# Retention attention feeding a GELU feed-forward layer: two units per attention block, q/k transposes by DMA, state summed in SBUF, initial loads reordered

## The chip, the cores and the metric

The kernel runs on one core of one Trainium2 chip. The metric is the device time of one execution in microseconds. The core has the engines PE (TensorE matmul, with its weight loads shown apart as PEld), DVE (VectorE), ACT (ScalarE), POOL (GpSimd) and SP (SyncE). In this kernel POOL and SP mostly issue DMAs.

## The reference, cut to what matters

```python
# q, k, v: batch 8, heads 8, sequence 576, head width 64
scores = scale * q @ k.T                        # per batch and head
gamma  = 1 - 2 ** (-5 - head)
Dmat   = where(i >= j, gamma ** (i - j), 0)     # decay, causal
attn   = (scores * Dmat) @ v
x = attn.transpose(0, 2, 1, 3).reshape(4608, 512)
h = x @ w_in                                    # 512 -> 2048
out = (h * sigmoid(1.702 * h)) @ w_out          # 2048 -> 512
```

The decay splits into a factor of the row and a factor of the column, so a sequence can be worked off in pieces of 128 positions: within a piece by masked scores, and from all earlier pieces through a running state, the sum of k times the scaled v.

## The kernel before, in words

**Units and chunks.** The 4608 rows are cut into 36 units of 128 rows (`NU`). Nine units make two batches: units 0 to 3 are pieces 0 to 3 of the first batch (kind 0), units 4 to 7 those of the second (kind 1), and the ninth holds the last 64 positions of both (kind 2). Four units are one chunk of 512 rows for the feed-forward part, so there are 9 chunks.

**One unit of attention.** `load_qk` and `load_v` bring k, q (cast to bf16 on the way) and v (fp32) to SBUF in rows of positions; all are issued from POOL. `scale_v` (DVE, L284) multiplies v by the column's decay into `vp`. `transposes` (L293) turns k and q with eight 128x128 transposes on PE into the PSUM bank `psT`, and one DVE copy (L296) brings them to `qkT`. `state` (L305) adds the four head pairs' k-v products to the bank `psK`, where they accumulate over the pieces of a batch; `state_out` (L315) multiplies the bank by a block-diagonal mask `bdm` into `kv`. `inter` (L326, or L332 for the ninth units) multiplies q by that state into `psO`; it is absent for the first piece of a batch. `scores` (L342) makes the eight heads' scores with half-height (64-row) matmuls into two banks `psS`, `scores_out` (L350) masks them into `pm`, `values` (L359) adds `pm` times `vp` to `psO` with half-width (64-column) matmuls, and `values_out` (L368) applies the row's decay and writes 128 columns of `xT`.

**Feed-forward.** `up` (L374) is four 512-column matmuls and a GELU on ACT (L379) into `gT`; 16 of them make a chunk. `down` (L392) is four 512-column matmuls, a quarter of one unit's output; after four of them `down_out` copies the bank on ACT (L401) to `osb` and SP stores it.

**Order.** Every engine takes its instructions in program order; `Program` adds the semaphore waits. One loop step `t` deals with one unit: state of unit `t`, transposes of `t+2`, inter of `t`, scores of `t+1`, values of `t`, then four `up` groups of an earlier chunk and four `down` groups of a still earlier one (`LAG` = 12 steps behind), one of each in turn. The first `up` is at step 4, the first `down` at step 12. POOL issues the loads in this order: k, q, v of units 0 to 3, and then alternately a quarter of `w_in` and the three loads of one further unit, and later `w_out`.

Of the kernel before, what the change touches and what calls it, by code (L numbers as in the profile page):

```python
# [7 lines left out]
ALU = mybir.AluOpType  # L8
# [5 lines left out]
P = 128  # L14
# [5 lines left out]
LAG = 12  # L20
# [121 lines left out]
def bass_retnet_parallel__then__act_gelu_quick_kernel(  # L142
# [8 lines left out]
    NLD = 8  # L151
    es = ExitStack()
    with es:
# [10 lines left out]
        bdm = sb("bdm", [P, P], BF16)  # L164
# [6 lines left out]
        qn = [sb(f"qn{i}", [P, H, DH], BF16) for i in range(NLD)]  # L171
        kn = [sb(f"kn{i}", [P, H, DH], BF16) for i in range(NLD)]
        vn = [sb(f"vn{i}", [P, H, DH], FP32) for i in range(NLD)]
        vp = [sb(f"vp{i}", [P, H, DH], BF16) for i in range(3)]
        qkT = [sb(f"qkT{i}", [P, 2 * HP, P], BF16) for i in range(3)]
        pm = [[sb(f"pm{i}_{hh}", [P, HP, P], BF16) for hh in range(2)] for i in range(2)]
        kv = [[sb(f"kv{i}_{j}", [P, HP, P], BF16) for j in range(2)] for i in range(2)]
# [3 lines left out]
        gT = [sb(f"gT{i}", [P, NF, 512], BF16) for i in range(4)]  # L181
        osb = [sb(f"osb{i}", [P, DM], FP32) for i in range(4)]

        psT = ps("psT", [P, 2 * HP, P], BF16)
        psS = [ps(f"psS{hh}", [P, HP, P]) for hh in range(2)]
        psO = ps("psO", [P, HP, P])
        psK = ps("psK", [P, HP, P])
        psH = [ps(f"psH{i}", [P, 512]) for i in range(2)]
        psY = ps("psY", [P, 512])
# [4 lines left out]
        def load_qk(u):  # L194
            sl = u % NLD
            rows = unit_rows(u)
            for src, dst, nm in ((k, kn[sl], "kn"), (q, qn[sl], "qn")):
                def f(e, src=src, dst=dst):
                    return [
                        e.dma_start(  # L200
                            dst[p0 : p0 + n, :, :],
                            src[b, :, s0 : s0 + n, :].rearrange("h p d -> p h d"),
                        )
                        for p0, n, b, s0 in rows
                    ]
                op("pool", f, writes=[f"{nm}{sl}"], dma=f"d_{nm}{sl}", ndma=len(rows))

        def load_v(u):
# [11 lines left out]
            op("pool", f, writes=[f"vn{sl}"], dma=f"d_vn{sl}", ndma=len(rows))  # L220
# [13 lines left out]
        def setup():  # L234
# [3 lines left out]
            op("pool", lambda e: e.iota(  # L238
                iota_c.ap(), [[1, S]], base=0, channel_multiplier=0,
                allow_small_or_imprecise_dtypes=True), writes=["iota_c"])  # L240
            op("pool", lambda e: e.iota(
                iota_k.ap(), [[128, 5]], base=0, channel_multiplier=1,
                allow_small_or_imprecise_dtypes=True), writes=["iota_k"])
            op("dve", lambda e: e.tensor_scalar_add(
                iota_k[64:128, 4:5], iota_k[64:128, 4:5], -64.0),
               reads=["iota_k"], writes=["iota_k"])
            op("dve", lambda e: e.tensor_single_scalar(ident.ap(), dmat.ap(), 0.0, ALU.is_equal),  # L247
               reads=["dmat"], writes=["ident"])
            op("dve", lambda e: e.tensor_single_scalar(mask.ap(), dmat.ap(), 0.0, ALU.is_ge),
               reads=["dmat"], writes=["mask"])  # L250
            op("dve", lambda e: e.tensor_single_scalar(maskc.ap(), dmat.ap(), 0.0, ALU.is_ge),
               reads=["dmat"], writes=["maskc"])
            op("dve", lambda e: e.memset(maskc[0:64, 64:128], 0.0), reads=["maskc"], writes=["maskc"])
            op("dve", lambda e: e.memset(bdm.ap(), 0.0), writes=["bdm"])
            op("dve", lambda e: e.memset(bdm[0:64, 0:64], 1.0), reads=["bdm"], writes=["bdm"])
            op("dve", lambda e: e.memset(bdm[64:128, 64:128], 1.0), reads=["bdm"], writes=["bdm"])
            op("dve", lambda e: e.memset(lnsc.ap(), math.log(QK_SCALE)), writes=["lnsc"])
            for hp in range(HP):
                for hh in range(2):
                    op("dve", lambda e, hp=hp, hh=hh: e.memset(  # L260
                        lng[64 * hh : 64 * hh + 64, hp : hp + 1], math.log(gamma(2 * hp + hh))),
                       writes=[f"lng{hp}_{hh}"])
            for h in range(H):
# [18 lines left out]
        def scale_v(u):  # L282
            sl, _, ty = u % NLD, *unit_info(u)[1:]
            op("dve", lambda e: e.tensor_tensor(  # L284
                vp[u % 3].ap(), vn[sl].ap(),
                vfac[:, ty, :, None].to_broadcast([P, H, DH]), ALU.mult),
               reads=[f"vn{sl}"] + VF, writes=[f"vp{u % 3}"])

        def transposes(u):
            sl = u % NLD  # L290
            for t, (src, nm) in enumerate(((kn[sl], "kn"), (qn[sl], "qn"))):
                for hp in range(HP):
                    op("pe", lambda e, src=src, hp=hp, t=t: e.matmul(  # L293
                        psT[:, (1 - t) * HP + hp, :], src[:, 2 * hp : 2 * hp + 2, :], ident.ap(),
                        is_transpose=True), reads=[f"{nm}{sl}", "ident"], writes=["psT"])
            op("dve", lambda e: e.tensor_copy(qkT[u % 3].ap(), psT.ap()),  # L296
               reads=["psT"], writes=[f"qkT{u % 3}"])

        def state(u):
# [3 lines left out]
            sl = u % NLD  # L303
            for hp in range(HP):
                op("pe", lambda e, hp=hp: e.matmul(  # L305
                    psK[:, hp, :], kn[sl][:, 2 * hp : 2 * hp + 2, :],
                    vp[u % 3][:, 2 * hp : 2 * hp + 2, :],
                    start=(c == 0 and hp == 0), stop=True, skip_group_check=True),
                   reads=[f"kn{sl}", f"vp{u % 3}"], writes=["psK"])

# [206 lines left out]
```

## Time and profile before

| what | value |
|---|---|
| time, median of 3 runs (range) | 338.47 us (338.08 to 339.63) |
| the profiled execution | 338.57 us, its span 336.7 us |
| PE busy | 316.9 us, 94% of the span |
| DVE, ACT, POOL busy | 132.6, 115.4, 108.5 us |
| first `up` on PE | 33.80 us |
| end of the last matmul | 332.8 us |
| chain that ended last | PE 89%, POOL 6%, DMA 3% |

The profile is of one execution. The span runs from the first to the last recorded instruction; the time is 1.9 us longer. Matmuls are pipelined, so the length of one matmul says less than the distance from one start to the next.

### The profile page before, as it was taken

How to read it: one execution, taken by the hardware profiler on the slowest of the kernel's cores; microseconds unless marked ns; L12 is line 12 of the kernel's file. 1: busy time of each engine (PE TensorE's matmuls, PEld its weight loads, DVE VectorE, ACT ScalarE, POOL GpSimd, SP SyncE). 2: the span in 40 equal slices, each digit the busy share in tenths (PEclk: the TensorE clock that was granted, in tenths of full speed). 3: DMA queues.
4: the chain of work that ended last, by engine and by line, in shares of the span. 5: the costliest groups of instructions: out<-in, count | busy, mean ns of one | idle time of the engine just before them, and what ended most of it. 6: DMA issues, size and time to landing. Idle time of an engine off the chain costs nothing.

```text
span 336.7 us, 5221 instructions
## 1 busy us (share of the span) xinstructions
PE 316.9 (94%) x2272; PEld 162.5 (48%) x2272; DVE 132.6 (39%) x229; ACT 115.4 (34%) x198; POOL 108.5 (32%) x135
## 2 busy tenths in 40 slices
PE   1676999999999999999999999999999999999995
PEld 0444455555555555555555555555555544443442
DVE  2687766864444434444444434444443200000000
ACT  5400345443333333333333333333333344442211
POOL 8999976842322514222322604000000000000000
PEclk9999999999999999999999999999999999999999
DMA  9999999996666907667666907001000001011122
GB/s 83 190 196 218 215 210 214 221 202 88 98 88 86 153 31 98 91 95 93 95 93 94 158 31 95 31 33 31 33 31 33 31 34 62 31 33 62 62 94 64
DMA packets 87447, 32.85 MB, mean 98 GB/s; under 512 B 76416, under 2 KB 80512, under 8 KB 87424
## 3 DMA queue, kind: packets, MB, share of 16 engines
q0 software_dynamic: 82176, 23.08, 60.3%
q1 hardware_dynamic: 5248, 9.44, 8.1%
q8 instruction: 18, 0.29, 0.4%
q14 instruction: 5, 0.04, 0.0%
HBM read 36.70 MB, written 9.44 MB: 137 GB/s over the span
## 4 chain that ended last, share of the span: by engine, by line
PE 89%; POOL 6%; DMA 3%; ACT 0%; issue 0%; POOLq 0%
PE psH L374 38%; PE psY L392 31%; PE psS L392 4%; PE psT L293 4%; PE psO L359 3%; DMA qn<-in_q_dram 3%; PE psS L342 3%; PE psO L392 2%; POOL kn L200 2%; PE psK L305 2%; POOL vn L214 2%; POOL qn L200 2%; PE psO L326 1%; POOL w_in_sb L223 1%; ACT osb L401 0%; PE psO L332 0%
## 5 line engine op out<-in xcount | busy, mean ns | idle before, releaser
L379 ACT ACTIVATE gT<-psH 128x512 bf16<-128x512 f32 x144 | 86.0, 597 | 182.9 <-PE psH L374 182.9
L374 PE MATMUL psH<-xT,w_in_sb 128*128 128x512 bf16 x576 | 145.1, 381 | 0.0
L392 PE MATMUL psY<-w_out_sb,gT 128*128 128x512 bf16 x480 | 122.2, 379 | 0.7 <-ACT osb L401 0.7
L374 PEld LDWEIGHTS psH<-xT,w_in_sb 128*128 128x128 bf16 x576 | 52.6, 98 | 65.4 <-ACT gT L379 5.1
L392 PEld LDWEIGHTS psY<-w_out_sb,gT 128*128 128x128 bf16 x480 | 46.5, 98 | 57.9 <-ACT osb L401 2.4
L296 DVE COPY qkT<-psT 128x1024 bf16<-128x1024 bf16 x36 | 24.8, 690 | 108.0 <-PE psT L293 107.9
L200 POOL DMA_DIRECT2D kn<-in_k_dram x40 | 36.8, 928 | 94.8 <-PE psK L305 80.3
L214 POOL DMA_DIRECT2D vn<-in_v_dram x40 | 37.4, 947 | 2.5 <-issue 2.4
L200 POOL DMA_DIRECT2D qn<-in_q_dram x40 | 37.0, 935 | 0.0
L284 DVE TENSOR_TENSOR vp<-vn,vfac 128x512 bf16<-128x512 f32 x36 | 24.6, 685 | 13.9 <-DMA vn<-in_v_dram 13.9
L368 DVE TENSOR_TENSOR xT<-psO,gq 128x512 bf16<-128x512 f32 x36 | 24.5, 680 | 6.0 <-PE psO L359 6.0
L293 PE MATMUL psT<-ident,kn 128*128 128x128 bf16 x144 | 15.5, 236 | 11.3 <-DVE ident L247 5.2
L401 ACT ACTIVATE osb<-psY 128x512 f32<-128x512 f32 x30 | 17.9, 597 | 14.0 <-PE psY L392 14.0
L350 DVE TENSOR_TENSOR pm_1<-psS,mask 128x512 bf16<-128x512 f32 x32 | 21.8, 680 | 0.0
L350 DVE TENSOR_TENSOR pm_0<-psS,mask 128x512 bf16<-128x512 f32 x32 | 21.8, 680 | 0.0
L293 PE MATMUL psT<-ident,qn 128*128 128x128 bf16 x144 | 15.5, 236 | 1.5 <-DMA qn<-in_q_dram 1.5
L293 PEld LDWEIGHTS psT<-ident,kn 128*128 128x128 bf16 x144 | 10.4, 105 | 13.3 <-DMA kn<-in_k_dram 8.6
L359 PE MATMUL psO<-pm_1,vp 128*64 128x128 bf16 x144 | 15.9, 237 | 0.0
L359 PE MATMUL psO<-pm_0,vp 128*64 128x128 bf16 x144 | 15.9, 237 | 0.0
L342 PE MATMUL psS<-qkT 64*128 64x128 bf16 x288 | 15.6, 233 | 0.0
L305 PE MATMUL psK<-vp,kn 128*128 128x128 bf16 x128 | 13.5, 233 | 2.0 <-DVE kv_0 L315 1.4
L305 PEld LDWEIGHTS psK<-vp,kn 128*128 128x128 bf16 x128 | 10.0, 103 | 9.6 <-DVE kv_0 L315 1.9
(44 smaller groups left out, 140.3 us busy)
## 6 DMA issues: line engine op xcount, KB each, us to landing
vn<-in_v_dram POOLq DMA_DIRECT2D x32, 256.0 KB, 5.0
out_dram<-osb SPq DMA_DIRECT2D x32, 256.0 KB, 2.0
kn<-in_k_dram POOLq DMA_DIRECT2D x32, 128.0 KB, 4.5
qn<-in_q_dram POOLq DMA_DIRECT2D x32, 128.0 KB, 5.2
w_in_sb<-in_moe_w_in_dram POOLq DMA_DIRECT2D x4, 512.0 KB, 10.1
w_out_sb<-in_moe_w_out_dram POOLq DMA_DIRECT2D x4, 512.0 KB, 15.5
vn<-in_v_dram POOLq DMA_DIRECT2D x8, 128.0 KB, 6.3
out_dram<-osb SPq DMA_DIRECT2D x8, 128.0 KB, 2.4
```

The lines of the kernel that those rows point to most:

```text
L200: e.dma_start(dst[p0 : p0 + n, :, :], src[b, :, s0 : s0 + n, :].rearrange("h p d -> p h d"),)
L214: e.dma_start(vn[sl][p0 : p0 + n, :, :], v[b, :, s0 : s0 + n, :].rearrange("h p d -> p h d"),)
L284: op("dve", lambda e: e.tensor_tensor(vp[u % 3].ap(), vn[sl].ap(), vfac[:, ty, :, None].to_broadcast([P, H, DH]), ALU.mult), reads=[f"vn{s ...
L293: op("pe", lambda e, src=src, hp=hp, t=t: e.matmul(psT[:, (1 - t) * HP + hp, :], src[:, 2 * hp : 2 * hp + 2, :], ident.ap(), is_transpose= ...
L296: op("dve", lambda e: e.tensor_copy(qkT[u % 3].ap(), psT.ap()), reads=["psT"], writes=[f"qkT{u % 3}"])
L305: op("pe", lambda e, hp=hp: e.matmul(psK[:, hp, :], kn[sl][:, 2 * hp : 2 * hp + 2, :], vp[u % 3][:, 2 * hp : 2 * hp + 2, :], start=(c == 0 ...
L342: op("pe", lambda e, hp=hp, hh=hh: e.matmul(psS[hh][:, hp, :], qt[64 * hh : 64 * hh + 64, HP + hp, :], qt[64 * hh : 64 * hh + 64, hp, :], ...
L350: op("dve", lambda e, hh=hh: e.tensor_tensor(pm[u % 2][hh].ap(), psS[hh].ap(), m[:, None, :].to_broadcast([P, HP, P]), ALU.mult), reads=[f ...
L359: op("pe", lambda e, hp=hp, hh=hh: e.matmul(psO[64 * hh : 64 * hh + 64, hp, :], vp[u % 3][:, 2 * hp + hh, :], pm[u % 2][hh][:, hp, :], sta ...
L374: op("pe", lambda e, a=a: e.matmul(psH[n % 2].ap(), w_in_sb[:, a, P * f : P * f + P], xT[c % 3][:, a, :], start=(a == 0), stop=(a == HP - 1)),
L379: op("act", lambda e: e.activation(gT[c % 4][:, f, :], psH[n % 2].ap(), AF.Gelu_apprx_sigmoid), reads=[f"psH{n % 2}"], writes=[f"gT{c % 4} ...
L392: op("pe", lambda e, f=f: e.matmul(y, gT[c % 4][:, f, P * r : P * r + P], w_out_sb[:, f, :], start=(f == 0), stop=(f == NF - 1)), reads=[f ...
```

## The change

Units 0 to 7 get an attention of their own (`attend`), one unit after the other with all its steps in a row: units 0 to 3 before the first chunk's 16 `up`, units 4 to 7 between that chunk and the next. In these the transposes stay on PE and the copy alternates between DVE (even units) and ACT (odd units). From unit 8 on, `block(m)` takes two units at a time, `2m` and `2m+1`: both `inter`, then the `scores` of the next two units, then both `values`. The transposes of units 8 to 35 are one DMA each, from SBUF to SBUF, issued by SP two blocks ahead (`ready`). k and q share the tile `kq`. The state is no longer accumulated in PSUM: each piece's product goes to a bank of its own, and DVE adds its two diagonal halves to an fp32 sum `kvf` in SBUF and copies that to `kv` in bf16 (`state`); the off-diagonal parts of the eight `kv` tiles are zeroed once at the start. Between blocks a written-out plan of eight `up` and eight `down` groups is run, with the states of the two units after next at its fourth and seventh `up`. v is loaded from SP, and the order of the first loads is k and q of units 0 to 3, all of `w_in`, k and q of units 4 to 7, then `w_out`, while the v loads on SP wait for named earlier loads. Banks and buffers are renamed and counted anew. In `scores` the two units of a pair use banks `S0`, `S1` and `S2`, `S3`; `S0` and `S2` also take `down`'s output, and `S1` the states.

```diff
-LAG = 12
...
+    NQT = 10
+    NVP = 6
+    NPE = 8
...
-        bdm = sb("bdm", [P, P], BF16)
...
-        qn = [sb(f"qn{i}", [P, H, DH], BF16) for i in range(NLD)]
-        kn = [sb(f"kn{i}", [P, H, DH], BF16) for i in range(NLD)]
+        kq = [sb(f"kq{i}", [P, 2, DM], BF16) for i in range(NLD)]
         vn = [sb(f"vn{i}", [P, H, DH], FP32) for i in range(NLD)]
-        vp = [sb(f"vp{i}", [P, H, DH], BF16) for i in range(3)]
-        qkT = [sb(f"qkT{i}", [P, 2 * HP, P], BF16) for i in range(3)]
-        pm = [[sb(f"pm{i}_{hh}", [P, HP, P], BF16) for hh in range(2)] for i in range(2)]
-        kv = [[sb(f"kv{i}_{j}", [P, HP, P], BF16) for j in range(2)] for i in range(2)]
+        vp = [sb(f"vp{i}", [P, H, DH], BF16) for i in range(NVP)]
+        qkT = [sb(f"qkT{i}", [P, 2 * HP, P], BF16) for i in range(NQT)]
+        pm = [[sb(f"pm{i}_{hh}", [P, HP, P], BF16) for hh in range(2)] for i in range(4)]
+        kvf = [sb(f"kvf{i}", [P, HP, DH], FP32) for i in range(2)]
+        kv = [[sb(f"kv{i}_{j}", [P, HP, P], BF16) for j in range(4)] for i in range(2)]
...
-        gT = [sb(f"gT{i}", [P, NF, 512], BF16) for i in range(4)]
+        gT = [sb(f"gT{i}", [P, NF, 512], BF16) for i in range(3)]
...
-        psT = ps("psT", [P, 2 * HP, P], BF16)
-        psS = [ps(f"psS{hh}", [P, HP, P]) for hh in range(2)]
-        psO = ps("psO", [P, HP, P])
-        psK = ps("psK", [P, HP, P])
-        psH = [ps(f"psH{i}", [P, 512]) for i in range(2)]
-        psY = ps("psY", [P, 512])
+        banks = {n: ps(f"ps{n}", [P, 512]) for n in ("H0", "H1", "O0", "O1", "S0", "S1", "S2", "S3")}
+
+        def by_pair(n):
+            return banks[n].ap().rearrange("p (a b) -> p a b", b=P)
...
+        def load_v(u, after=()):
...
-            op("pool", f, writes=[f"vn{sl}"], dma=f"d_vn{sl}", ndma=len(rows))
+            op("sp", f, reads=after, writes=[f"vn{sl}"], dma=f"d_vn{sl}", ndma=len(rows))
...
+            for i in range(2):
+                for j in range(4):
+                    op("dve", lambda e, i=i, j=j: e.memset(kv[i][j].ap(), 0.0), writes=[f"kv{i}_{j}"])
...
+        def transpose_pe(u, bank):
             sl = u % NLD
-            for t, (src, nm) in enumerate(((kn[sl], "kn"), (qn[sl], "qn"))):
-                for hp in range(HP):
-                    op("pe", lambda e, src=src, hp=hp, t=t: e.matmul(
-                        psT[:, (1 - t) * HP + hp, :], src[:, 2 * hp : 2 * hp + 2, :], ident.ap(),
-                        is_transpose=True), reads=[f"{nm}{sl}", "ident"], writes=["psT"])
-            op("dve", lambda e: e.tensor_copy(qkT[u % 3].ap(), psT.ap()),
-               reads=["psT"], writes=[f"qkT{u % 3}"])
-
-        def state(u):
+            t = banks[bank].ap().bitcast(BF16).rearrange("p (a b) -> p a b", b=P)
+            for j in range(2 * HP):
+                op("pe", lambda e, j=j: e.matmul(
+                    t[:, j, :], kq[sl][:, j // HP, P * (j % HP) : P * (j % HP) + P], ident.ap(),
+                    is_transpose=True), reads=[f"kq{sl}_{j // HP}", "ident"], writes=[bank])
+            if u % 2:
+                op("act", lambda e: e.activation(qkT[u % NQT].ap(), t, AF.Copy),
+                   reads=[bank], writes=[f"qkT{u % NQT}"])
+            else:
+                op("dve", lambda e: e.tensor_copy(qkT[u % NQT].ap(), t),
+                   reads=[bank], writes=[f"qkT{u % NQT}"])
+
+        def transpose_dma(u):
+            sl = u % NLD
+            op("sp", lambda e: e.dma_start_transpose(
+                qkT[u % NQT].ap(), kq[sl].ap().rearrange("p a b -> p (a b)")),
+               reads=[f"kq{sl}_0", f"kq{sl}_1"], writes=[f"qkT{u % NQT}"],
+               dma=f"d_qkT{u % NQT}")
...
+        def state(u, bank="S1"):
             pb, kind, c = unit_info(u)
             if kind == 2:
                 return
             sl = u % NLD
+            kb = by_pair(bank)
             for hp in range(HP):
                 op("pe", lambda e, hp=hp: e.matmul(
-                    psK[:, hp, :], kn[sl][:, 2 * hp : 2 * hp + 2, :],
-                    vp[u % 3][:, 2 * hp : 2 * hp + 2, :],
-                    start=(c == 0 and hp == 0), stop=True, skip_group_check=True),
-                   reads=[f"kn{sl}", f"vp{u % 3}"], writes=["psK"])
-
-        def state_out(u):
-            pb, kind, c = unit_info(u)
-            if kind == 2:
-                return
-            op("dve", lambda e: e.tensor_tensor(
-                kv[kind][c % 2].ap(), psK.ap(), bdm[:, None, :].to_broadcast([P, HP, P]), ALU.mult),
-               reads=["psK", "bdm"], writes=[f"kv{kind}_{c % 2}"])
+                    kb[:, hp, :], kq[sl][:, 0, P * hp : P * hp + P],
+                    vp[u % NVP][:, 2 * hp : 2 * hp + 2, :],
+                    start=(hp == 0), stop=True, skip_group_check=True),
+                   reads=[f"kq{sl}_0", f"vp{u % NVP}"], writes=[bank])
+            for hh in range(2):
+                r = slice(64 * hh, 64 * hh + 64)
+                dst, acc, src = kv[kind][c][r, :, r], kvf[kind][r], kb[r, :, r]
+                kvk, kfk = f"kv{kind}_{c}_{hh}", f"kvf{kind}_{hh}"
+                if c == 0:
+                    op("dve", lambda e, d=acc, s=src: e.tensor_copy(d, s), reads=[bank], writes=[kfk])
+                elif c < 3:
+                    op("dve", lambda e, d=acc, s=src: e.tensor_tensor(d, s, d, ALU.add),
+                       reads=[bank, kfk], writes=[kfk])
+                if c < 3:
+                    op("dve", lambda e, d=dst, s=acc: e.tensor_copy(d, s),
+                       reads=[kfk, f"kv{kind}_{c}"], writes=[kvk])
+                else:
+                    op("dve", lambda e, d=dst, s=src, a=acc: e.tensor_tensor(d, s, a, ALU.add),
+                       reads=[bank, kfk, f"kv{kind}_{c}"], writes=[kvk])
...
+        def attend(u, tbank, kbank):
+
+            scale_v(u)
+            transpose_pe(u, tbank)
+            state(u, kbank)
+            scores(u)
+            scores_out(u, 0)
+            scores_out(u, 1)
+            inter(u)
+            values(u)
+            values_out(u)
+
+        def fetch(m):
+            for u in (2 * m, 2 * m + 1):
+                if u < NU:
+                    load_kq(u)
+                    load_v(u)
+
+        def ready(m):
+            for u in (2 * m, 2 * m + 1):
+                if u < NU:
+                    scale_v(u)
+                    transpose_dma(u)
+
+        def block(m):
+
+            a, b = 2 * m, 2 * m + 1
+            nxt = 2 * m + 2 < NU
+            inter(a)
+            inter(b)
+            if nxt:
+                scores(a + 2)
+                scores(b + 2)
+                scores_out(a + 2, 0)
+            values(a)
+            values(b)
+            values_out(a)
+            values_out(b)
+            if nxt:
+                scores_out(a + 2, 1)
+                scores_out(b + 2, 0)
+                scores_out(b + 2, 1)
+            fetch(m + 4)
+            ready(m + 2)
+
+        def states(m, i):
+            u = 2 * m + (i == 6)
+            if i in (3, 6) and u < NU:
+                state(u)
+
+        YB = ("S0", "S2")
+
+        load_kq(0)
         setup()
         load_v(0)
         for u in range(1, 4):
-            load(u)
+            load_kq(u)
+            load_v(u, [f"kq{u - 1}_1"])
         for i in range(4):
             load_win(i)
-            load(4 + i)
-        nh = 0
-        for t in range(-2, NU + LAG):
-            if t + 2 < NU:
-                scale_v(t + 2)
-            if 0 <= t < NU:
-                state(t)
-            if t + 2 < NU:
-                transposes(t + 2)
-            if 0 <= t < NU:
-                state_out(t)
-                inter(t)
-                if t < 4:
-                    load_wout(t)
-                load(t + NLD)
-            if 0 <= t + 1 < NU:
-                scores(t + 1)
-                scores_out(t + 1)
-            if 0 <= t < NU:
-                values(t)
-                values_out(t)
-            ch, hq = divmod(t - 4, 4)
-            co, r = divmod(t - LAG, 4)
-            bank = "psY"
-            if t >= NU + 4:
-                bank = ("psY", "psS0", "psS1", "psO")[t % 4]
-            for s in range(4):
-                if 0 <= ch < NCH:
-                    up(ch, 4 * hq + s, nh)
-                    nh += 1
-                if 0 <= co < NCH:
-                    down(co, r, s, bank)
-            if 0 <= co < NCH:
-                down_out(co, r, bank)
+        for u in range(4, 8):
+            load_kq(u)
+            load_v(u, [f"win{2 + (u > 5)}"])
+        for u in range(4):
+            attend(u, "H0", "H1")
+        for i in range(4):
+            load_wout(i)
+        fetch(4)
+        for f in range(16):
+            up(0, f)
+        for u in range(4, 8):
+            attend(u, "O0", "S3")
+        ready(4)
+        fetch(5)
+        for f in range(16):
+            up(1, f)
+            states(4, f - 8)
+        ready(5)
+        scores(8)
+        scores(9)
+        for u in (8, 9):
+            for hh in range(2):
+                scores_out(u, hh)
+        fetch(6)
+        for i in range(8):
+            down(0, i, ("S0", "S2"))
+        fetch(7)
+        block(4)
+        for i in range(8, 16):
+            down(0, i, ("S0", "S2"))
+            states(5, i - 8)
+        for m in range(5, NU // 2 + 1):
+            if m < NU // 2:
+                block(m)
+            c, h = divmod(m - 1, 2)
+            plan = "DDUUDUDUDUDUDUDU"
+            iu = idn = 0
+            for x in plan:
+                if x == "D":
+                    down(c - 1, 8 * h + idn, YB)
+                    idn += 1
+                else:
+                    up(c, 8 * h + iu)
+                    iu += 1
+                    states(m + 1, iu - 1)
+        for i in range(16):
+            down(NCH - 1, i, ("S0", "S2", "O0", "O1"))
```

## Prediction

> **What bounds the kernel now.** I read first the slices of the span, then PE's timeline in a middle step, then its start.
>
> ```profile
> PE   1676999999999999999999999999999999999995
> DMA  9999999996666907667666907001000001011122
> ```
>
> PE is full from the fifth slice to the last. The first four (33.7 us) have gaps, and there the DMA engines are full. So the time is a start plus a PE sum. A middle step:
>
> ```profile
> 99.07 0.39 PE L305 MATMUL psK<-vp,kn 128*128 128x128 bf16 x4
> 99.30 0.39 PE L293 MATMUL psT<-ident,kn 128*128 128x128 bf16 x4
> 99.52 0.39 PE L293 MATMUL psT<-ident,qn 128*128 128x128 bf16 x4
> 99.74 0.39 PE L326 MATMUL psO<-qkT,kv_1 128*128 128x128 bf16 x4
> 100.06 0.40 PE L342 MATMUL psS<-qkT 64*128 64x128 bf16 x8
> 100.39 0.24 PE L359 MATMUL psO<-pm_0,vp 128*64 128x128 bf16 x1
> ...
> 100.74 0.60 PE L374 MATMUL psH<-xT,w_in_sb 128*128 128x512 bf16 x2
> ```
>
> Read start to start. Four full 128-column matmuls take 0.22 us. Eight scores, two at a time, take as long plus a gap of 0.10 before and 0.11 after; eight values 0.22 plus 0.13. So a unit costs 1.67 us: state, inter, scores, values 0.22 each, transposes 0.44, three gaps 0.34. The feed-forward of the step lay from 92.16 to 99.07: 6.91 for 32 matmuls, 0.216 each. A step is 8.58 us and waits for nothing. The start:
>
> ```profile
> 9.26 0.61 PE L293 MATMUL psT<-ident,kn 128*128 128x128 bf16 x4 [2.60 <-DVE qkT L296]
> 9.94 0.61 PE L293 MATMUL psT<-ident,qn 128*128 128x128 bf16 x4
> 10.47 0.61 PE L342 MATMUL psS<-qkT 64*128 64x128 bf16 x8
> ...
> 33.80 4.47 PE L374 MATMUL psH<-xT,w_in_sb 128*128 128x512 bf16 x16
> 38.11 0.39 PE L305 MATMUL psK<-vp,kn 128*128 128x128 bf16 x4
> ```
>
> Here four matmuls take 0.61 with their drain instead of 0.39: PE runs at half pace, although the granted-clock row shows 0.9 or more everywhere. The first 16 `up` take 4.31 against 3.46: 0.86 us to get warm.
>
> Check of the sum: 33.8 + 1152 x 0.2159 (248.7) + 28 states (6.2) + 29 transposes (12.8) + 25 inters (5.5) + 30 scores (6.6) + 31 values (6.8) + 31 x 0.34 (10.5) + 0.86 = 331.8; PE really ended at 332.8, 0.3% of the sum later. Then 3.9 us of last copy and store: span 336.7; the profiled execution lasted 338.57, 1.87 more, and is 0.1 us above the median of 338.47.
>
> **The steady part, gained.** From unit 8 on the eight transposes go (0.44), and two units share three gaps (0.17 a unit). A block with its plan is 64 x 0.216 + 8 x 0.22 + 0.34 = 15.9 us against 17.2. For 28 units that is 17.1 us off the path. I give back 0.1 us a block: the first `down` writes `S0`, which scores_out frees about 1.73 us after the block's start (inters 0.44, gap, scores and drain to 0.97, then DVE 0.68 and a signal), and PE arrives at 1.63; bounds 0 to 0.2. Nothing else is late: `xT` is written 3.0 us after the block's start, and the first `up` that reads it comes at 3.4.
>
> DVE loses a 0.61 copy and a 0.60 state_out per unit, and gains four half-height 256-column pieces. No row shows one. The rows around them:
>
> ```profile
> L315 DVE TENSOR_TENSOR kv_1<-psK,bdm 128x512 bf16<-128x512 f32 x16 | 10.9, 681 | 5.0 <-PE psK L305 5.0
> L251 DVE TENSOR_SCALAR maskc<-dmat 128x128 bf16<-128x128 f32 x1 | 0.2, 207 | 0.0
> ```
>
> By columns an add is about 0.42 us, a copy 0.27, and each copy waits 0.08 for its add (as the memsets of `bdm` do), so 1.4 us per unit; bounds 0.8 (all as short as 0.2) to 2.7 (all as long as 0.68). In a block of 15.9 us DVE then has 8 us of work: hidden. It is not hidden in the first eight units.
>
> Moved at no cost: v's issue (0.95 us each) leaves POOL, whose queue only shortens. On SP it waits for the scale_v eight units back, long done; behind it stand transposes and stores, and a late store first holds the ACT copy four units on, a cover of two blocks. The three `gT` (four before) are free a chunk ahead. If such a cover went, ACT's GELU and then PE would wait.
>
> **The start, lost.** In `attend` a unit's steps follow one another. From the end of a unit's second mask, cold: values 0.06 to 0.70 us; values_out on DVE at 0.73, next scale_v at 1.33, the qkT copy at 1.93 (DVE) or 1.67 to 2.69 (ACT, 1.02 from its 0.60 per 512 columns), state on PE done at 2.68, state pieces 2.71 to 4.07, two masks to 5.35. The loop is 5.35 us, 4.67 for the fourth piece (two pieces). Unit 0's second mask ends at 11.2: `ident` at 4.2, masks and eight memsets on DVE to 7.2, scale, copy and pieces to 10.0. So values of unit 3 end at 27.3, its values_out at 28.0, and the first `up` is at 28.1. The loads don't hold this up: before, q of unit 2 had landed at 13.6, 4.2 MB (four units, `w_in`) take 20 us at the 214 GB/s of the full slices, and `w_in` is first needed at 28. The closest is v of unit 1: SP holds it until q of unit 0 has landed, about 7, and with the 5.0 of its row it is there at 12.0, needed at 12.6; each us later would cost one, bounds 0 to 2, I take 0. Against the old 33.8 that is 5.7 earlier, but the old order had 2.8 us more attention behind it.
>
> Then 16 `up`: 13.8 + 0.86, to 42.8. Units 4 to 7 now stand alone on PE, which needs 6.7 for them: the same loop, with two waits more: the transposes of 5 and 7 share `O0` with values_out of 4 and 6, and scores of 5 and 7 share `S3` with the state pieces. Walked through it is 22.8 us cold, 20.3 with PE warm. Whether PE stays warm here no row tells: all stutter on record (5 to 33 us) begins cold, this begins after 14.7 us of dense work. I take the middle, 21.5: 64.3. The next 16 `up` and a state: 14.0 and half of 0.86, 78.8.
>
> The Trainium skill's page "TensorE: Matmul & The Clock Gate", section "Why this matters for your kernels", says that the clock falls back after idle gaps above about 3 us. My walk's longest gap is 2.2 us, so by that rule PE would stay warm and the sum below would be 1.7 lower.
>
> Scores of 8 and 9 with the wait for their first mask 1.3, eight `down` 6.9, block 4 1.4, eight `down` and two states 7.4: 95.8. Rest: 960 matmuls 207.3, 21 states, 21 inters, 24 scores, 26 values at 0.22 20.2, 13 x 0.34 4.4, 13 x 0.1 1.3, and 0.3% 0.8: 234.1. PE ends at 329.9; +3.9 span 333.8; +1.87 **335.7 us**, 0.8% faster.
>
> **The transposing DMAs.** No row shows one. Two are issued by SP about a block before use, behind v loads and stores that no longer wait by then, so what counts is whether a pair lands in 15.9 us. Nearest rows:
>
> ```profile
> vn<-in_v_dram POOLq DMA_DIRECT2D x32, 256.0 KB, 5.0
> out_dram<-osb SPq DMA_DIRECT2D x32, 256.0 KB, 2.0
> ```
>
> A transpose moves 256 KB: 2.0 us if it goes like the store on the same queue, 5.0 like the v load in 256-byte pieces. If it broke into 32-byte pieces, 8192 at queue 0's 39.5 ns (60.3% of 16 engines' span over 82176 packets) would be 20.2 us. I take 5, a pair in 10, hidden; a block takes over 15.9 only from 8 us each.
>
> "VectorE: DVE Perf Modes" in the Trainium skill, section "The three transpose paths", speaks against the change: it gives 1309 ns per 128x128 by DMA against 390 ns on TensorE. Eight in a row would by it be an estimated 10.5 us a unit and 21 a pair, a total near 402. "DMA: Bandwidth & Descriptors", section "Latency and other measured facts", has 261 GB/s for a transpose by DMA, an estimated 1 us a unit, and nothing would be late.
>
> **Rivals.** (1) All bounds kind: PE warm (-1.7), pieces 0.8 (-3.4 over six units), no wait at `S0` (-1.3): 329 to 331. For it: bounds above; against: all three are needed. (2) Slower, one mechanism: a half-height piece costs as much as a full row. In `attend` the pieces stand between state and masks: +1.35 for six units, +0.5 for two, +9: 345. It decides from 1.85 us a unit: 6 x 0.45 and 2 x 0.1 are the 2.9 us that my sum gains. For it: the first TENSOR_SCALAR of 128 columns took 673 ns. Against: L251's 207. (3) Slower: transposes late. Each us of a pair above 15.9 counts in 13 blocks; at 9 us each it is +27, 363. For it: the unknown piece size; against: even the 256-byte row leaves 6 us.
>
> **How the numbers follow.** 0.5% (1.7 us) is about what a measurement here can tell. Forecast 0.58, spanning 333 (warm) to 338.5 (cold and some delay): faster 0.37, same 0.18, slower 0.03. Rival 1 0.11, all faster. Rival 2 0.20: 0.03 same, 0.17 slower. Rival 3 0.11, slower. Together faster 0.48, same 0.21, slower 0.31. The range 330 to 346 leaves out rival 3 and a little of rival 1.
>
> **What would show it.** Right: first `up` near 28; units 4 to 7 taking 20 to 23 us with PE half empty; from there blocks of 15.9 us without waits on qkT; PE busy down by 17. Wrong: PE waiting for a DMA before scores (rival 3); an attend loop above 6 us with pieces near 0.68 (rival 2); a block much longer than 16 us for any other reason.

## The result and the profile after

The changed kernel takes 351.18 us (median of 4 runs, 348.15 to 352.40) against 339.04 for the kernel before beside it: 1.035 times as long, 95% interval 1.028 to 1.042. The forecast was 335.7 us with a range of 330 to 346: wrong in its sign, and the time lies outside the range. Every ratio in this document is formed from the executions that lie within 1.5% of the fastest one of the same kernel. The profiled execution took 351.04 us, its span is 349.2.

First the slices of the changed kernel's page:

```profile
PE   2546976689795999999999999999999999999995
PEclk9999996579997899999999999999999999999999
DMA  9999999994569689999797999999540410100022
```

And from the trace's list of DMA issues (count, then the median us from issue to landing) the row that the trace before did not have:

```profile
qkT<-kq SPq DMA_TRANSPOSE x28, 5.2
```

PE has gaps not in four slices but in ten of the first thirteen (a slice is 8.7 us), up to about 113 us, and the granted clock falls to 0.5 to 0.7 in slices 7 to 9 and to 0.7 and 0.8 in slices 13 and 14; before, it stood at 0.9 or more in every slice. A DMA transpose takes 5.2 us from issue to landing (3.1 to 11.8). From the chain of waits, the first down groups of three consecutive blocks far from the start:

```profile
145.91 1.89 PE psS L416 x8
...
161.68 1.89 PE psS L416 x8
...
177.45 1.89 PE psS L416 x8
```

A block is 15.8 us. Ten blocks from 129.91 to 288.52 are 15.86 each, against 2 x 8.58 = 17.16 before. So the steady part gains what it was forecast to gain, and the whole loss lies before 130 us. The steps of the prediction beside the trace, from one start on PE to the next:

| step | predicted, us | measured, us |
|---|---|---|
| first `up` at | 28.1 | 32.85 |
| 16 `up` of chunk 0 | 14.7 | 16.0 |
| units 4 to 7 | 21.5 | 22.95 |
| 16 `up` of chunk 1 and a state | 14.5 | 15.6 |
| scores of 8 and 9, to the first `down` | 1.3 | 2.8 |
| eight `down`; block 4; eight `down` | 15.7 | 16.0 |
| block 5, to its first `down` | 1.6 | 6.2 |
| plan behind block 5 | 14.3 | 15.9 |
| the rest of PE | 218.2 | 216.9 |
| PE ends at | 329.9 | 345.3 |

The lines behind the large differences, from PE's timeline of the changed kernel (start, length, what; in brackets the idle time before it and what ended it):

```profile
32.85 16.18 PE L403 MATMUL psH<-xT,w_in_sb 128*128 128x512 bf16 x64 [0.79 <-DVE xT L392]
48.87 0.61 PE L292 MATMUL psO<-ident,kq 128*128 128x128 bf16 x8
...
52.73 0.24 PE L382 MATMUL psO<-pm_0,vp 128*64 128x128 bf16 x1 [2.07 <-DVE pm_0 L372]
...
71.82 14.61 PE L403 MATMUL psH<-xT,w_in_sb 128*128 128x512 bf16 x60 [0.79 <-DVE xT L392]
...
90.26 7.08 PE L416 MATMUL psS<-w_out_sb,gT 128*128 128x512 bf16 x32 [1.72 <-DVE pm_0 L372]
...
108.90 0.56 PE L364 MATMUL psS<-qkT 64*128 64x128 bf16 x8 [2.00 <-DMA qkT<-kq]
110.98 0.61 PE L364 MATMUL psS<-qkT 64*128 64x128 bf16 x8 [1.52 <-DMA qkT<-kq]
```

From DVE's timeline of the same kernel, unit 1's state pieces, what unit 2 waited for, and what stood ahead of the masks of unit 8:

```profile
14.27 0.42 DVE L328 TENSOR_TENSOR kvf<-psH,kvf 64x256 f32<-64x256 f32 x1 [0.70 <-PE psH L316]
14.72 0.37 DVE L331 CAST kv_1<-kvf 64x256 bf16<-64x256 f32 x1
15.11 0.43 DVE L328 TENSOR_TENSOR kvf<-psH,kvf 64x256 f32<-64x256 f32 x1
15.57 0.40 DVE L331 CAST kv_1<-kvf 64x256 bf16<-64x256 f32 x1
15.99 0.69 DVE L372 TENSOR_TENSOR pm_0<-psS,mask 128x512 bf16<-128x512 f32 x1
...
21.73 0.69 DVE L283 TENSOR_TENSOR vp<-vn,vfac 128x512 bf16<-128x512 f32 x1 [3.04 <-DMA vn<-in_v_dram]
...
88.20 1.29 DVE L283 TENSOR_TENSOR vp<-vn,vfac 128x512 bf16<-128x512 f32 x2
89.51 0.69 DVE L372 TENSOR_TENSOR pm_0<-psS,maskc 128x512 bf16<-128x512 f32 x1
```

And SP's queue around block 5:

```profile
94.55 3.81 SPq L430 DMA_DIRECT2D out_dram<-osb  x2
98.40 4.90 SPq L213 DMA_DIRECT2D vn<-in_v_dram  x5
103.40 3.02 SPq L304 DMA_TRANSPOSE qkT<-kq  x2
```

The reader is to see four things. v of unit 2 came 3.0 us late. Units 4 to 7 leave PE waiting, mostly for DVE, from 48.9 to 71.8. The first `down` waited for a mask that was itself queued on DVE behind two scale_v (1.3 us). And the transposes of units 12 and 13 were issued at 103.4 us only, behind two stores and five v loads on SP (the issue of the five alone took 4.9 us), while PE came for them at 106.7.

### The profile page after: what moved, and what is told of

Same layout as the page of the kernel before. It is cut to its first block, busy times and chain, and to the rows that moved or that the text cites. A ratio compares the mean times of both kernels' runs of the same rounds, so it can differ in the third digit from the quotient of the medians.

```text
span 349.2 us, 4899 instructions
## 1 busy us (share of the span) xinstructions
PE 311.4 (89%) x2048; PEld 153.6 (44%) x2048; DVE 138.1 (40%) x282; ACT 119.4 (34%) x202; POOL 74.6 (21%) x95
## 4 chain that ended last, share of the span: by engine, by line
PE 80%; DMA 8%; DVE 6%; SPq 2%; POOL 2%; issue 1%; ACT 1%; POOLq 0%
PE psH L403 37%; PE psS L416 33%; DMA vn<-in_v_dram 4%; PE psO L382 3%; PE psS L364 2%; PE psO L416 2%; DMA qkT<-kq 2%; PE psS L316 2%; DMA kq<-in_q_dram 2%; SPq L213 1%; POOL kq L199 1%; DVE pm_0 L372 1%; PE psO L346 1%; DVE xT L392 1%; DVE pm_1 L372 1%; DVE vp L283 1%
## 5 line engine op out<-in xcount | busy, mean ns | idle before, releaser
L416 PE MATMUL psS<-w_out_sb,gT 128*128 128x512 bf16 x544 | 136.0, 383 | 1.7 <-DVE pm_0 L372 1.7
L416 PEld LDWEIGHTS psS<-w_out_sb,gT 128*128 128x128 bf16 x544 | 51.4, 98 | 60.1 <-DVE pm_0 L372 3.0
L199 POOL DMA_DIRECT2D kq<-in_k_dram x40 | 35.3, 889 | 162.4 <-PE psS L316 160.9
L199 POOL DMA_DIRECT2D kq<-in_q_dram x40 | 34.7, 875 | 3.5 <-issue 3.5
L424 ACT ACTIVATE osb<-psS 128x512 f32<-128x512 f32 x34 | 20.3, 597 | 32.0 <-PE psS L416 32.0
L392 DVE TENSOR_TENSOR xT<-psO,gq 128x512 bf16<-128x512 f32 x36 | 23.5, 684 | 14.7 <-PE psO L382 14.7
L328 DVE TENSOR_TENSOR kvf<-psS,kvf 64x256 f32<-64x256 f32 x28 | 11.8, 422 | 37.4 <-PE psS L316 37.1
L382 PE MATMUL psO<-pm_0,vp 128*64 128x128 bf16 x144 | 15.8, 245 | 8.3 <-DVE pm_0 L372 8.0
L382 PEld LDWEIGHTS psO<-pm_0,vp 128*64 128x64 bf16 x144 | 10.2, 120 | 11.8 <-DVE pm_0 L372 10.3
L364 PEld LDWEIGHTS psS<-qkT 64*128 64x128 bf16 x288 | 9.4, 101 | 10.7 <-issue 4.5
L316 PE MATMUL psS<-vp,kq 128*128 128x128 bf16 x112 | 11.5, 229 | 0.4 <-DVE vp L283 0.4
L316 PEld LDWEIGHTS psS<-vp,kq 128*128 128x128 bf16 x112 | 8.9, 103 | 6.3 <-DVE vp L283 0.7
## 6 DMA issues: line engine op xcount, KB each, us to landing
w_in_sb<-in_moe_w_in_dram POOLq DMA_DIRECT2D x4, 512.0 KB, 12.1
```

What stands on the lines that cost most here:

```text
L199: e.dma_start(kq[sl][p0 : p0 + n, i, :].rearrange("p (h d) -> p h d", d=DH), src[b, :, s0 : s0 + n, :].rearrange("h p d -> p h d"),)
L316: op("pe", lambda e, hp=hp: e.matmul(kb[:, hp, :], kq[sl][:, 0, P * hp : P * hp + P], vp[u % NVP][:, 2 * hp : 2 * hp + 2, :], start=(hp == ...
L328: op("dve", lambda e, d=acc, s=src: e.tensor_tensor(d, s, d, ALU.add), reads=[bank, kfk], writes=[kfk])
L364: op("pe", lambda e, hp=hp, hh=hh, bank=bank: e.matmul(by_pair(bank)[:, hp, :], qt[64 * hh : 64 * hh + 64, hp, :], qt[64 * hh : 64 * hh + ...
L382: op("pe", lambda e, hp=hp, hh=hh: e.matmul(ob[64 * hh : 64 * hh + 64, hp, :], vp[u % NVP][:, 2 * hp + hh, :], pm[u % 4][hh][:, hp, :], st ...
L392: op("dve", lambda e: e.tensor_tensor(xT[ch % 3][:, :, 128 * j : 128 * j + 128], by_pair(bank), gq[:, ty, :, :], ALU.mult), reads=[bank] + ...
```

## The experiments

Two theories stood against each other. A: the start costs the time, units 0 to 7 one after the other and a few wrong queue orders, while the DMA transposes gain. B: the transposing DMAs cost it.

### e1_petr: the transposes back on PE

```diff
         def ready(m):
             for u in (2 * m, 2 * m + 1):
                 if u < NU:
                     scale_v(u)
-                    transpose_dma(u)
...
             if i in (3, 6) and u < NU:
                 state(u)
+            u = 2 * m + 2 + (i == 7)
+            if i in (5, 7) and u < NU:
+                transpose_pe(u, "S3")
...
             up(1, f)
+            if f in (4, 6):
+                transpose_pe(8 + (f == 6), "S3")
```

> The changed kernel, with the transposes of units 8 to 35 put back on PE: two per plan, eight 128-column matmuls each into bank S3, copied by DVE or ACT. Everything else stays, so this prices the DMA transposes alone. Theory A (the loss is in the start, where units 0 to 7 go one after the other; the DMA transposes themselves gain): PE gets 28 x 0.44 = 12.3 us more, and the wait for qkT at block 5 (4.6 us in the trace of the changed kernel) with the half-pace stretch behind it (1.7) goes: 6 us slower than the changed kernel, about 357. Theory B (the transposing DMAs are what costs, by waits and by crowding the DMA engines): no slower than the changed kernel, 351 or less. Blocks: 16.8 us by A.

Measured: 364.98 us, 1.076 times the kernel before (1.070 to 1.081), 13.8 more than the changed kernel. A block, from PE's timeline, with the wait inside it:

```profile
182.09 1.90 PE L416 MATMUL psS<-w_out_sb,gT 128*128 128x512 bf16 x8
...
198.57 0.40 PE L364 MATMUL psS<-qkT 64*128 64x128 bf16 x8 [0.38 <-ACT qkT L296]
...
199.47 0.82 PE L416 MATMUL psS<-w_out_sb,gT 128*128 128x512 bf16 x3
```

17.38 us a block instead of 15.86: the transposes' 0.88, and 0.4 to 0.6 of waiting for a copy on ACT that my placing of the second transposes left too little time, so this prices the DMA transposes too high. Over 13 blocks that wait is an estimated 5 to 8 of the 13.8 us, so 6 or more are left without it. B falls: without the DMA transposes the kernel is slower.

### e2_early: the transposes of units 12 and 13 ahead of the first stores

```diff
         fetch(6)
+        ready(6)
         for i in range(8):
             down(0, i, ("S0", "S2"))
...
             fetch(m + 4)
-            ready(m + 2)
+            if m > 4:
+                ready(m + 2)
```

> The changed kernel, with the scale and the transposing DMAs of units 12 and 13 put in program order ahead of the first eight down groups instead of inside block 4, so that on SP they stand ahead of the first two stores. If block 5 waits only because SP was held by those stores (its two transposes were issued at 103.4 and needed at 106.7), the wait goes: 4.6 us, and the half-pace plan behind it 1.7: about 345. If the transposes are late for the loads' or the transfer's sake, the wait stays and the time is 351.

Measured: 346.33 us, ratio 1.021 (1.015 to 1.027), 4.9 less than the changed kernel. In PE's timeline block 5's scores now follow without a wait:

```profile
92.14 8.64 PE L416 MATMUL psS<-w_out_sb,gT 128*128 128x512 bf16 x32 [1.72 <-DVE pm L372]
...
110.27 0.71 PE L364 MATMUL psS<-qkT 64*128 64x128 bf16 x16
```

The wait was SP's order, as expected. Here the eight `down` behind the mask wait ran partly at half pace (8.5 us to the next instruction instead of 6.9), which takes back 1.6 of the 6.3 expected. The transposes now stand ahead of the stores and of the v loads behind them both, so it is SP's queue above, not this run, that tells the two apart: stores until 98.4, v loads until 103.3.

### e3_spread: units 4 to 7 between chunk 0's up groups

```diff
-        for f in range(16):
-            up(0, f)
-        for u in range(4, 8):
-            attend(u, "O0", "S3")
+        scale_v(4)
+        for f in range(16):
+            u, j = 4 + f // 4, f % 4
+            if j == 0:
+                transpose_pe(u, f"O{u % 2}")
+            if j == 2:
+                scores(u)
+                scores_out(u, 0)
+                scores_out(u, 1)
+                state(u, f"S{3 - 2 * (u % 2)}")
+                if u < 7:
+                    scale_v(u + 1)
+            if j == 0 and u > 4:
+                inter(u - 1)
+                values(u - 1)
+                values_out(u - 1)
+            up(0, f)
+        inter(7)
...
```

> The changed kernel, with units 4 to 7 no longer after chunk 0's 16 up groups but spread between them: transposes, two up groups, scores and state, two up groups, inter and values with the next unit's transposes. The work is the same. Theory A: the 23 us in which PE is two thirds idle shrink to the 6.7 that it needs, and the second start from a cold clock (1.2 us) goes: 17 us less, about 334. Rival (the loads of units 4 to 7 and of w_out hold the start whatever the order, since the DMA engines are full to 80 us): less than 6 us gained, 345 or more, and PE waits for loads between the up groups.

Measured: 339.08 us, ratio 0.999 (0.996 to 1.002): 12.1 less than the changed kernel, the whole loss, by reordering four units. Two waits became longer (PE's timeline):

```profile
33.11 3.59 PE L403 MATMUL psH<-xT,w_in_sb 128*128 128x512 bf16 x8
...
56.16 13.13 PE L403 MATMUL psH<-xT,w_in_sb 128*128 128x512 bf16 x60 [0.79 <-DVE xT L392]
...
75.09 8.62 PE L416 MATMUL psS<-w_out_sb,gT 128*128 128x512 bf16 x32 [3.69 <-DVE pm L372]
...
96.78 0.61 PE L364 MATMUL psS<-qkT 64*128 64x128 bf16 x8 [3.51 <-DMA qkT<-kq]
```

From 33.1 to 56.2 now lie chunk 0's 16 `up` and units 4 to 7, which took 39.0 us before. They take 23.05 now: 15.9 us gained, and 1.5 more because chunk 1's `up` start warm. Some 4.5 are given back (first `down` 2.0, the eight `down` that then ran partly at half pace 1.5, block 5 1.0), because everything behind comes sooner to v of unit 11, on which DVE waits 1.8 us, and to SP's late transposes.

### e5_vpool: v of the first eight units on POOL

```diff
-        load_v(0)
+        load_v(0, eng="pool")
...
-            load_v(u, [f"kq{u - 1}_1"])
+            load_v(u, eng="pool")
...
-            load_v(u, [f"win{2 + (u > 5)}"])
+            load_v(u, eng="pool")
```

> The changed kernel, with v of the first eight units loaded from POOL right behind its k and q, as before the change, instead of from SP behind a wait. In the trace of the changed kernel v of unit 2 was used at 21.7 after a wait of 3.0 us and v of unit 3 after 0.5, and the first up stood at 32.9 where the walk had 28.1. If the waits on SP and the sharing with w_in made v late: first up 3.5 to 4.8 us earlier, about 347. If the DMA engines were simply full: no difference, 351. POOL gets 0.95 us of issue per unit more, by which w_in comes 4 us later: without effect before 28 us.

Measured: 349.49 us, ratio 1.031 (1.025 to 1.037). The first `up` stands at 30.67 instead of 32.85 in the traces; the medians differ by 1.7 us, less than their intervals can tell apart. In the traces of e1_petr, e2_early and e8_warm, which have the changed kernel's start, it stands at 33.5 to 33.8, so these 2.2 us are no accident of one execution. Issued from POOL, without SP's waits and ahead of `w_in`, v came sooner by about half of what I had missed at the first `up`; which of the two had held it, the run does not tell.

### e8_warm: PE kept busy in units 4 to 7

```diff
+        def idle_pe(n):
+            for a in range(n):
+                op("pe", lambda e, a=a: e.matmul(
+                    banks["H0"].ap(), w_in_sb[:, a % HP, 0:P], xT[0][:, a % HP, :],
...
             scores_out(u, 1)
+            if u >= 4:
+                idle_pe(6)
             inter(u)
             values(u)
+            if u >= 4:
+                idle_pe(2)
             values_out(u)
```

> The changed kernel, with eight useless 512-column matmuls a unit into the free bank H0 in units 4 to 7: six (1.3 us) where PE waits for the masks, two before values_out. No work is left out. Theory: the clock falls in these units because PE is busy too small a share of the time, though no gap is above 2.1 us. Then with the filling the granted clock stays at 1.0 from 49 to 72 us, the units take 21 us or less instead of 23.0, and the next 16 up start warm (1.2 us): 347 to 348. Rival (the clock falls for another reason, or the filling delays what it is to help): the clock falls all the same and the time is 351 or more.

Measured: 345.51 us, ratio 1.022 (1.017 to 1.027): 5.7 less than the changed kernel by 32 matmuls more. The stages of the changed kernel first (columns: stretch, its length, busy time of PE, PEld, DVE, ACT, POOL with counts, granted clock, DMA share, GB/s):

```profile
48.00:54.00 6.00, 2.75 (x33) 1.63 (x32) 3.88 (x8) 1.19 (x2) 1.75 (x2) 1.00 1.36 188
54.00:60.00 6.00, 4.06 (x35) 2.80 (x36) 3.95 (x9) 1.02 (x1) 1.76 (x2) 0.53 2.40 155
60.00:66.00 6.00, 3.45 (x32) 2.04 (x29) 5.07 (x11) 0.00 (x0) 1.75 (x2) 0.50 1.78 156
```

Then those of this kernel:

```profile
54.00:60.00 6.00, 4.71 (x49) 2.54 (x50) 4.15 (x9) 1.02 (x1) 1.75 (x2) 1.00 2.37 156
60.00:66.00 6.00, 4.70 (x48) 2.54 (x47) 5.40 (x11) 0.00 (x0) 1.75 (x2) 1.00 1.82 158
```

The clock column goes from 0.50 to 1.00. The units take 21.3 us (49.5 to 70.8) instead of 22.95, chunk 1's `up` start at full pace (1.5 us), and the granted clock stays at 1.00 in every later stretch. These two make 3.1 of the 5.7 us. The rest came later: block 5 waited less, and the plan behind it ran at full pace (PE's timeline):

```profile
107.89 0.40 PE L364 MATMUL psS<-qkT 64*128 64x128 bf16 x8 [2.57 <-DMA qkT<-kq]
...
108.79 1.90 PE L416 MATMUL psS<-w_out_sb,gT 128*128 128x512 bf16 x8
```

The length of one gap did not decide: in the changed kernel no gap from 49 to 54 us is above 2.1 us, and the clock fell at about 54; here PE stood idle for 2.57 us in block 5 and went on at full pace. The filling raised PE's busy share and shortened the gaps as well, so the run does not separate these two.

### e6_order: e3_spread with two queue orders put right

```diff
-        ready(5)
+        ready(5, "t")
         scores(8)
         scores(9)
...
+        ready(5, "s")
         fetch(6)
+        ready(6, "t")
         for i in range(8):
             down(0, i, ("S0", "S2"))
...
             fetch(m + 4)
-            ready(m + 2)
+            ready(m + 2, "st" if m > 4 else "s")
```

In `ready`, "t" stands for the transposing DMAs alone and "s" for the scale alone.

> Units 4 to 7 spread between chunk 0's up groups, as in e3_spread, and two orders put right: the transposing DMAs of units 12 and 13 stand on SP ahead of the first two stores, and the scale of units 10 and 11, which waited for its v load 3.4 us and held the masks of unit 8 behind it on DVE, comes after the masks of units 8 and 9. In e3_spread the first down group waited 3.7 us for that mask and block 5 waited 4.5 us for its transposes, and the plan behind each ran 1.3 to 1.6 us at half pace. If these waits are queue orders: 3 + 1.5 + 4.5 + 1.3 = 10 us less than 339, about 329. Rival (the loads are late, the DMA engines being full until 80 us): the waits move to the next user of the same load, and 336 to 339 is measured.

Measured: 329.82 us, ratio 0.973 (0.968 to 0.977), 9.3 less than e3_spread. The first `down` waits 0.5 us instead of 3.7 and block 5 not at all; new are a wait of 1.0 for the transpose of unit 11 in block 4 and, in block 6, waits of 0.7 and 1.0 for those of units 14 and 15, behind which the first eight matmuls of `down` took 2.9 us to the next instruction instead of 1.7 (PE's timeline):

```profile
71.60 7.08 PE L416 MATMUL psS<-w_out_sb,gT 128*128 128x512 bf16 x32 [0.52 <-DVE pm L372]
...
80.27 0.40 PE L364 MATMUL psS<-qkT 64*128 64x128 bf16 x8 [1.02 <-DMA qkT<-kq]
...
89.07 0.71 PE L364 MATMUL psS<-qkT 64*128 64x128 bf16 x16
...
105.68 0.40 PE L364 MATMUL psS<-qkT 64*128 64x128 bf16 x8 [0.74 <-DMA qkT<-kq]
```

So the queue orders held what was expected of them, and the rival has a small part: some 3 us of waiting and half pace moved to block 6. The wait on v in e3_spread was 1.8 us by its trace, not 3.4; the two scales themselves took 1.4.

### e7_best: the start of units 0 to 3 too

```diff
             transpose_pe(u, tbank)
-            state(u, kbank)
             scores(u)
             scores_out(u, 0)
             scores_out(u, 1)
+            state(u, kbank)
             inter(u)
...
-            load_v(u, [f"kq{u - 1}_1"])
+            load_v(u, eng="pool")
...
-        for i in range(4):
-            load_wout(i)
         fetch(4)
+        for i in range(4):
+            load_wout(i)
```

> e6_order and three more: v of the first eight units on POOL behind its k and q (e5_vpool gained 2.2 us at the first up), k and q of units 8 and 9 ahead of w_out, and in units 0 to 3 the state pieces on DVE behind the two masks instead of ahead of them, so that they run while PE makes the values: 0.7 us a unit. Expected 2.2 + 2.5 = 5 us less than e6_order, about 324, below both kernels. If DVE bounds units 0 to 3 (4.7 us of work each), the last gains nothing and it is 327.

Measured: 325.64 us (325.20 to 325.95), ratio 0.962 (0.959 to 0.965): 13 us below the kernel before and 25 below the changed one, with all four parts of the change in it, though the order of the first loads is partly another. Values of unit 3 end at 26.8 us, but the first `up` is at 32.5 (PE's timeline):

```profile
31.24 0.61 PE L293 MATMUL psO<-ident,kq 128*128 128x128 bf16 x4 [4.41 <-DMA kq<-in_k_dram]
...
32.49 2.91 PE L404 MATMUL psH<-xT,w_in_sb 128*128 128x512 bf16 x8
```

k of unit 4, loaded behind all of `w_in`, is what PE now waits for.

### e9_trbefore: one part alone, in the kernel before

```diff
+        def transposes_dma(u):
+            sl = u % NLD
+            for t, (src, nm) in enumerate(((kn[sl], "kn"), (qn[sl], "qn"))):
+                op("sp", lambda e, src=src, t=t: e.dma_start_transpose(
+                    qkT[u % 6][:, (1 - t) * HP : (2 - t) * HP, :],
...
-            if t + 2 < NU:
+            if t + 2 < 12:
                 transposes(t + 2)
+            if 12 <= t + 4 < NU:
+                transposes_dma(t + 4)
```

> The kernel before, with one part of the change alone: the transposes of units 12 to 35 by DMA from SP (two of 128x512 a unit, issued four steps before the unit, six qkT buffers). Units 0 to 11 stay on PE. If the DMA transposes gain what PE no longer does: 24 x 0.44 = 10.5 us less, 328; steps of 8.1 us instead of 8.6. Rival (they cost by waits or by crowding the loads): 335 or more, and PE waits for qkT.

Measured: 329.84 us, ratio 0.973 (0.970 to 0.977), 8.8 less than before. A step, from PE's timeline:

```profile
131.34 0.39 PE L316 MATMUL psK<-vp,kn 128*128 128x128 bf16 x4
131.56 0.39 PE L337 MATMUL psO<-qkT,kv 128*128 128x128 bf16 x4
...
139.47 0.39 PE L316 MATMUL psK<-vp,kn 128*128 128x128 bf16 x4
```

8.13 us instead of 8.58, with nothing between state and inter: the transposes' 0.44 is gone from PE, and no wait took its place. This is 0.44 of the 0.65 us a unit that the change gains in its steady part, and it needs no new order of the units. The DMA engines pay for it: from the list of DMA issues,

```profile
vn<-in_v_dram POOLq DMA_DIRECT2D x32, 256.0 KB, 15.2
...
qkT<-kn SPq DMA_TRANSPOSE x24, 9.2
```

a v load lands in a median of 15.2 us instead of 5.0, and the transposes of k in 9.2. Both are asked for steps ahead, and PE does not wait for them.

### e10_alt: the order of the first loads undone

```diff
         for i in range(4):
             load_win(i)
-        for u in range(4, 8):
-            load_kq(u)
-            load_v(u, eng="pool")
+            load_kq(4 + i)
+            load_v(4 + i, eng="pool")
```

> e7_best with the first loads in the order of the kernel before: a quarter of w_in and the loads of one further unit in turn, instead of all of w_in first. In e7_best values of unit 3 end at 26.8 us and then PE waits 4.4 us for k of unit 4, which stands behind w_in; the first up is at 32.5. With the old order k of unit 4 should land some 5 us earlier: first up at 28 to 29, 4 us less than e7_best, about 322. Rival (the DMA engines are full until 80 us, so what comes earlier here comes later there): a later quarter of w_in or a transpose of units 8 to 13 is waited for instead, and 325 to 326 is measured.

Measured: ratio 0.963 (0.958 to 0.969), no better than e7_best's 0.962; six executions lie from 324.8 to 330.8 us, and the profiled one took 325.17. PE's timeline shows the rival right:

```profile
27.52 2.07 PE L404 MATMUL psH<-xT,w_in_sb 128*128 128x512 bf16 x8
...
82.23 0.40 PE L365 MATMUL psS<-qkT 64*128 64x128 bf16 x8 [0.41 <-DMA qkT<-kq]
84.89 0.40 PE L365 MATMUL psS<-qkT 64*128 64x128 bf16 x8 [2.26 <-DMA qkT<-kq]
...
85.79 3.50 PE L417 MATMUL psS<-w_out_sb,gT 128*128 128x512 bf16 x8
```

The first `up` came 5.0 us earlier, and block 5 then waited 2.7 us for the transposes of units 12 and 13, with the plan behind it starting at half pace. The DMA engines are busy for 80% or more of every slice to this point in both kernels.

## Why the prediction was wrong

**The steady part was right.** 15.9 us a block was predicted and 15.86 measured; the rest of PE, 218.2 against 216.9. The transposing DMAs land in 5.2 us where I took 5.0 from the v load's row and not 2.0 from the store's, and rival 3 in its steady form (a pair above 15.9 us) did not happen.

**The step that failed most is "issued by SP about a block before use, behind v loads and stores that no longer wait by then".** For block 5 neither half holds. Between blocks 4 and 5 lie eight `down`, 7.4 us, not a plan of 14. And on SP the transposes stood behind two stores that had to wait for PE's `down` (94.6 to 98.4) and behind five v loads whose issue took another 4.9 us, the issue that the prediction had moved to SP "at no cost". Block 5 took 4.6 us longer (PE idle for 3.5, the rest mostly at half pace), and the plan behind it lost 1.6 to the clock: 6.2 of the 15.4 us by which PE ended later than predicted. e2_early shows the cause by taking the wait away.

**"The loads don't hold this up" failed for v of unit 2.** I had bounded unit 1's load and taken it at no delay; unit 2's was 3.0 us late and unit 3's 0.5. The state pieces took 1.58, 1.72 and 1.51 us in the first three units where I had 1.36, 0.7 together. These two make 4.2 of the 4.75 us at the first `up`. Rival 2, pieces as long as full rows, was wrong in its price: in those units an add or a copy took 0.42 or 0.43 us and a cast 0.28 to 0.40, not 0.68.

**The clock: I took the middle, it was cold.** Units 4 to 7 took 22.95 against 22.8 for the cold walk. The two starts from cold cost 2.2 and 1.5 us instead of 0.86 and half of it. Together these are 3.9 us.

**One wait was missed.** The masks of unit 8 stand on DVE behind the scale of units 10 and 11, which moved there by `ready(5)`; I had listed the wait for the mask, not the queue before it: 1.5 us, 1.3 of them the scale.

**The rule on idle gaps was not enough here.** The Trainium skill's page "TensorE: Matmul & The Clock Gate", section "Why this matters for your kernels", puts the danger at gaps above about 3 us. The trace has no gap above 2.1 us where the clock fell to 0.50, and filling the gaps kept it at 1.00 (e8_warm). The measurement decides.

**The price against DMA transposes did not decide.** By the 1309 ns per square of "VectorE: DVE Perf Modes", section "The three transpose paths", a unit would be an estimated 10.5 us, and the total near 402. In the changed kernel a unit lands in a median of 5.2 us. In e9_trbefore it comes near the estimate, 9.2 us for k and 9.5 for q, and yet the kernel gains 8.8 us, because PE is the bound and does not wait for them. The prediction's other estimate, 1 us a unit, was not seen: the shortest of the 28 took 3.1 us.

**The big term was in the sum, and too small.** The serial attention of units 4 to 7 was priced at 21.5 us against 6.7 that PE needs. That loss stood in the prediction; set against a gain of 17 it left a margin of 2.9 us, and five misses, all in the same direction, turned it over: 4.75 us at the first `up`, 3.9 by the clock, 1.5 at the mask, 4.6 at block 5 and 1.6 in the plan behind it (other steps gave back 1.0). The largest were waits in the queues of SP and of the loads, which my walk, made on PE and DVE, did not follow. My range allowed 10 us of delay in one place; 15 came in several.

## What to carry to other kernels

Price the start by walking every queue, SP's and the loads' too: here an order that is right in the middle of the kernel had half the lead at its beginning (7.4 us of `down` instead of a plan of 14). Moving work off the bound engine pays what the trace says (0.44 us a unit here), but the phase in which PE waited for others cost its length and the slow clock behind it, and spreading that work between dense work (e3_spread) gained the most of any single edit. Reordering the first loads, with the DMA engines full, moved the wait and did not remove it (e10_alt).

## What the runs showed of the hardware

- The granted TensorE clock halved with no idle gap above 2.1 us, in stretches where PE did about 1.7 us of full-pace work in 5.7, and stayed up when eight matmuls of 0.216 us a unit were added (e8_warm).
- After waits of 2.0 and 1.5 us in block 5 of the changed kernel the next eight matmuls, of two `down`, ran at half pace (3.35 us to the next instruction instead of 1.73). One wait of 1.7 us in e2_early cost 1.6 in the same way, yet in the changed kernel itself the same 1.7 us cost nothing, nor did one of 2.57 us in e8_warm.
- A transposing DMA of 128x1024 bf16 held SP's queue for 1.24 to 6.1 us, median 1.3, in the changed kernel. What stands behind it waits: in e6_order two of them held SP from 77.1 to 85.4, and the first store, whose four `down` had ended on PE at 75, was issued behind them.
- Transposing DMAs slow the loads beside them: with those of 24 units added in e9_trbefore, a v load landed in 15.2 us instead of 5.0 (medians).
